# Attention head of a fused attention and bilinear FFN kernel: loads of v taken from ScalarE's queue ahead of its first copy, and two casts of k given to VectorE

## The chip, the cores and the metric

The kernel runs on one core of a Trainium2 chip. The metric is the device time of one execution in microseconds (us); the kernel before has a median of 317.13 us over five runs (315.9 to 317.66). The engines are named as in the profile: PE is TensorE (PEld its weight loads), DVE is VectorE, ACT is ScalarE, POOL is GpSimd and SP is SyncE. SP and ACT each have a queue of their own on which they issue transfers; "SPq" and "ACTq" mark an issue.

## What is computed

Attention within chunks of 64 tokens, and a bilinear feed-forward network on what it gives:

```python
# q, k, v: (8 batches, 8 heads, 576 tokens, 64)
scores = scale * q_c @ k_c.T                  # per chunk of 64 tokens: 64 x 64
attn = exp(scores - max) / sum
out = attn @ v_c
x = out.transpose(0, 2, 1, 3).reshape(4608, 512)
return (x @ w_a) * (x @ w_b) @ w_out          # w_a, w_b: 512 x 1536; w_out: 1536 x 512
```

All inputs and the output are float32; the kernel multiplies in bf16.

## The kernel before

The 4608 tokens are cut into nine blocks of 512, and a block into two units of 256 tokens. The attention of a unit gives a slice of `xT` (512 features by 256 tokens, bf16). The FFN of a block K then runs over 12 slices of 128 hidden features: for each, four matmuls with `wb` and four with `wa` (L398), a copy of one product by ScalarE (L409) and the product of both by VectorE (L410). After the 12 slices come the output products (L420, or L479 with fewer multiplications from block 2 on). The attention of later units is threaded between the slices of earlier blocks. TensorE's order, and that of every engine, is the order in which the program is written (`manual_schedule`); nothing is moved by a scheduler.

The first block has nothing ahead of it to hide behind, so its attention is the head of the program, and it is written out by hand (L550 to L653). It is cut by heads, not by tokens: four pairs of heads m = 0 to 3, for all 512 tokens of the block. Unit 0 of the head holds heads 0 to 3 (pairs 0 and 1), unit 1 heads 4 to 7. For each pair:

- `load_quads(m, x, ...)` (L137; the transfer's line is L140) brings q (x = 0) or k (x = 1) of the pair, 256 KB in float32, into `f32`.
- `quad_cast(m, x, eng)` (L303, recorded at L169) casts it to bf16 in `qkb`, a tile of 128 x 512.
- `quad_turn(m, x, eng)` (L311) transposes it on TensorE (four matmuls, L317) into one of the four PSUM banks `F`, and `eng` copies it to `qkT` (ScalarE's copies are recorded at L167, the others at L169).
- `quad_scores(m)` (L331; L340) makes the scores in the PSUM tile `PS`, `expo(hu, mm)` (L245) their exponential in `E`.

For each unit, `half_sums` (L351) adds up the exponentials, `half_log` (L361) and `half_inverse` (L365) turn the sums into reciprocals on ScalarE, `half_values` (L374) multiplies with v, and `half_normalise` (L384) on VectorE writes `xT`. v is loaded by `load_half_v(hu, gs, eng)` (L145; L147), 128 KB for each of four groups g of 128 tokens, and cast on GpSimd by `cast_v` (L185; two pieces for unit 0, four for unit 1). The casts of the weights follow v's on GpSimd. `fill` (L535; L539) issues matmuls on zeros whose result is not used.

What sets the order around the change:

- ScalarE issues its transfers from the same instruction stream in which its copies and exponentials stand. Before, that stream is: four loads of k, the activation table, v of unit 0 for g = 1 and 3, the copy of pair 0's q (first evacuation), v of unit 1 for g = 1 and 3, the exponential of pair 0, the copy of pair 2's q, the exponential of pair 1, and so on. SyncE issues four loads of q, v of units 0 and 1 for g = 0 and 2, then the weights.
- Loads tell their end by eight semaphores taken in turn, in the order of the program text over both queues. A load that takes a semaphore again waits, in its engine's stream, until the load that held it has landed. So before, ScalarE's v loads wait for: k of pair 1 (g = 1), k of pair 2 (g = 3), and for unit 1 the second and third v load of SyncE. SyncE's four v loads wait for k and q of pair 0, q of pair 1 and q of pair 2.
- TensorE's scores of pair 1 wait for the exponential of pair 0 as well as for their own operands, because both pairs write the same PSUM tile.

Of the kernel before, what the change touches and what calls it, by code (L numbers as in the profile page):

```python
# [11 lines left out]
def kernel(  # L12
# [10 lines left out]
    nc = tc.nc  # L23
# [84 lines left out]
    def nextF():  # L108
        return ring("f", F)
# [35 lines left out]
    def load_half_v(hu, gs, eng):  # L145
        for g in gs:
            eng.dma_start(  # L147
                out=f32[hu][2][:, g * 256:(g + 1) * 256].rearrange("p (h d) -> p h d", h=4),
                in_=v[0, 4 * hu:4 * hu + 4, g * 128:(g + 1) * 128, :].transpose([1, 0, 2]),
            )  # L150
# [14 lines left out]
    def copy(eng, out, in_):  # L165
        if eng is nc.scalar:
            eng.copy(out=out, in_=in_)  # L167
        else:
            eng.tensor_copy(out=out, in_=in_)  # L169
# [15 lines left out]
    def cast_v(u, eng, pieces=1):  # L185
        n = 1024 // pieces
        for i in range(pieces):
            copy(eng, vb[u % 3][:, n * i:n * i + n], f32[u % NF32][2][:, n * i:n * i + n])
# [53 lines left out]
    def expo(u, h=None):  # L242
        e = E[u % 2]
        s = slice(0, 512) if h is None else slice(h * 256, h * 256 + 256)
        nc.scalar.activation(out=e[:, :, s], in_=PS[:, :, s], func=AF.Exp, scale=scale)  # L245
# [57 lines left out]
    def quad_cast(m, x, eng):  # L303
        c = (m % 2) * 512
        copy(
            eng,
            qkb[m // 2][:, x, c:c + 512].rearrange("p (r h d) -> p h r d", r=4, h=2),
            f32[m // 2][x][:, c:c + 512].rearrange("p (h r d) -> p h r d", h=2, r=4),
        )

    def quad_turn(m, x, eng):  # L311

        t = nextF().bitcast(BF16)
        c0 = (m % 2) * 512
        for r in range(4):
            c = r * 128
            nc.tensor.transpose(  # L317
                t[:, c:c + 128], qkb[m // 2][:, x, c0 + c:c0 + c + 128], identity
            )
        n = 8 * x + 4 * (m % 2)  # L320
        dst = qkT[m // 2][:, n:n + 4, :]
        if x == 0:
            copy(eng, dst, t[:, 0:512].rearrange("p (r t) -> p r t", r=4))
        else:
            copy(
                eng,
                dst.rearrange("p a b -> p (a b)").rearrange("p (t r) -> p t r", r=4),
                t[:, 0:512].rearrange("p (r t) -> p t r", r=4),
            )

    def quad_scores(m):  # L331
        hu, mm = m // 2, m % 2
        tq = qkT[hu][:, 4 * mm:4 * mm + 4, :]
        tk = qkT[hu][:, 8 + 4 * mm:12 + 4 * mm, :].rearrange("p a b -> p (a b)")
        for g in range(4):
            c = mm * 256 + g * 64
            for j in range(2):
                for cl in range(2):
                    n = 2 * g + cl
                    nc.tensor.matmul(  # L340
                        PS[cl * 64:cl * 64 + 64, j, c:c + 64].rearrange("p (t r) -> p r t", r=4),
                        tk[j * 64:j * 64 + 64, n * 64:n * 64 + 64],
                        tq[j * 64:j * 64 + 64, :, n * 16:n * 16 + 16],
                        start=True,
                        stop=True,
                    )
# [188 lines left out]
    def fill(times, bank=None, n=512):  # L535


        for _ in range(times):
            nc.tensor.matmul(  # L539
                PA[:, 0, 0:n] if bank is None else bank[:, 0:n],  # L540
                zero[:, 0:128],
                zero[:, 0:n],
                start=True,
                stop=True,
            )
# [4 lines left out]
    with tc.manual_schedule():  # L550
# [4 lines left out]
        V, A, G = nc.vector, nc.scalar, nc.gpsimd  # L555
# [7 lines left out]
                name=nc.get_next_instruction_name(), act_func_set_id=6, ins=[], outs=[]  # L563
            )
        )
        for hu in range(2):
            load_half_v(hu, (0, 2), nc.sync)
        load_half_v(0, (1, 3), nc.scalar)

        def queue_half(i, h):  # L570
            for n, src in (("b", moe_w_b), ("a", moe_w_a)):
# [28 lines left out]
        fill(2)  # L600
        quad_cast(0, 0, V)
        quad_turn(0, 0, A)
        load_half_v(1, (1, 3), nc.scalar)
        quad_cast(0, 1, V)
        quad_turn(0, 1, V)
        fill(1, n=128)
        for m in range(1, 4):
            for x in range(2):
                quad_cast(m, x, G)
        cast_v(0, G, 2)  # L610
        cast_v(1, G, 4)
        for h in range(2):
# [6 lines left out]
        quad_turn(2, 0, A)  # L619
        quad_scores(1)  # L620
        expo(0, 1)
        quad_turn(2, 1, V)
        quad_turn(3, 0, V)
        half_sums(0, PA)
# [269 lines left out]
```

## Time and profile before

| What | us |
|---|---|
| median of five runs | 317.13 (315.9 to 317.66) |
| the profiled execution | 318.66 |
| its span, first to last instruction | 316.9 |
| TensorE busy | 307.3, 97% of the span |
| VectorE, ScalarE, GpSimd busy | 185.9, 133.9, 124.7 |
| first exponential begins | 10.51 |
| first of the FFN's matmuls in the chain of waits | 20.85 |
| granted TensorE clock at half, in the head | 8.89 to 22.54 |

The profile is of one execution. A row of its timeline gives start and duration in us, engine and line, operation, the tiles written and read with their sizes, the count, and in brackets how long the engine had stood idle before and what released it. A row of the chain of waits gives start, duration and what ran. A row of the table by stretches gives the stretch, its length, the busy time of PE, PEld, DVE, ACT and POOL with counts, the granted clock (1.00 is full speed), the share of the DMA engines and GB/s.

### The profile page before, as it was taken

What the parts mean: (1) busy time and instruction counts of PE and PEld (TensorE: products, weight loads), DVE (VectorE), ACT (ScalarE), POOL (GpSimd) and SP (SyncE); (2) the same over time, 40 slices, a digit from 0 to 9 for tenths busy, and PEclk for the clock granted to TensorE, in tenths of its full rate; (3) what the DMA queues carried; (4) which work ended last, traced back from release to release, by engine and by line L of the source; (5) the groups of instructions that cost most, each with busy time, mean ns of one, the idle gap of its engine ahead of it and who ended that gap; (6) DMA issues with size and microseconds to landing.
All of it is one profiled execution on the core that took longest, in us unless ns stands there. A gap on an engine that the chain in (4) does not pass through costs nothing.

```text
span 316.9 us, 7288 instructions
## 1 busy us (share of the span) xinstructions
PE 307.3 (97%) x2902; PEld 179.0 (56%) x2902; DVE 185.9 (59%) x369; ACT 133.9 (42%) x227; POOL 124.7 (39%) x161
## 2 busy tenths in 40 slices
PE   5799999999999999999999999999999999999995
PEld 2544445784444477446744674467446744674474
DVE  2334434553536874977486758765876476646663
ACT  1543325744524551644164416451645164413320
POOL 3678868978352116600650065006600400040023
PEclk9559999999999999999999999999999999999999
DMA  7999999999999778999299439962700210021003
GB/s 261 325 383 396 373 262 225 234 265 266 210 199 258 168 168 207 221 256 241 107 243 235 91 84 210 222 153 99 168 2 0 92 46 0 3 92 40 2 0 133
DMA packets 145842, 55.00 MB, mean 174 GB/s; under 512 B 126224, under 2 KB 139792, under 8 KB 145808
## 3 DMA queue, kind: packets, MB, share of 16 engines
q1 hardware_dynamic: 142608, 52.97, 66.6%
q10 hardware_dynamic: 3200, 1.57, 1.7%
q8 instruction: 22, 0.36, 0.5%
q14 instruction: 12, 0.10, 0.1%
HBM read 37.75 MB, written 9.44 MB: 149 GB/s over the span
## 4 chain that ended last, share of the span: by engine, by line
PE 93%; ACT 2%; DMA 2%; POOL 0%; ACTq 0%; issue 0%; POOLq 0%; DVEq 0%; DVE 0%
PE F L398 60%; PE F L479 19%; PE F L420 6%; DMA f<-in_k_dram 2%; PE F L251 2%; PE PS L234 2%; PE PA L267 1%; PE F L539 1%; PE F L317 1%; ACT E L245 1%; ACT qkT L167 0%; POOL part L497 0%; PE PS L340 0%; ACT lns L277 0%; ACT inv L281 0%; ACT inv L365 0%
## 5 line engine op out<-in xcount | busy, mean ns | idle before, releaser
L398 PE MATMUL F<-xT,wb 128*128 128x512 bf16 (+1 forms) x460 | 113.1, 368 | 0.0
L398 PE MATMUL F<-xT,wa 128*128 128x512 bf16 (+1 forms) x460 | 112.9, 367 | 0.0
L409 ACT CAST bsb<-F 128x512 bf16<-128x512 f32 (+1 forms) x115 | 64.2, 559 | 107.0 <-PE F L398 106.8
L410 DVE TENSOR_TENSOR ab<-F,bsb 128x512 bf16<-128x512 f32 (+1 forms) x115 | 75.3, 656 | 51.9 <-PE F L398 44.2
L398 PEld LDWEIGHTS <-wa 128*128 128x128 bf16 x460 | 45.2, 98 | 48.9 <-issue 0.8
L398 PEld LDWEIGHTS <-wb 128*128 128x128 bf16 x460 | 43.7, 98 | 44.6 <-issue 0.7
L497 POOL TENSOR_TENSOR part<-part 128x256 f32<-128x256 f32 x14 | 10.2, 725 | 133.9 <-ACT part L523 132.9
L169 POOL CAST qkb<-f 128x1024 bf16<-128x1024 f32 (+1 forms) x37 | 35.8, 982 | 27.4 <-DMA f<-in_k_dram 16.6
L479 PEld LDWEIGHTS <-wst 128*128 128x128 bf16 x420 | 41.1, 98 | 4.7
L479 PE MATMUL F<-wst 128*128 128x256 bf16 x252 | 33.3, 273 | 0.0
L286 DVE TENSOR_TENSOR xT<-PA,inv 128x512 bf16<-128x512 f32 x32 | 21.8, 684 | 16.6 <-ACT inv L281 16.6
L497 DVE TENSOR_TENSOR osb<-F,part 128x256 f32<-128x256 f32 x56 | 22.3, 420 | 11.0 <-POOL part L497 9.4
L497 POOL TENSOR_TENSOR part<-part,osb 128x256 f32<-128x256 f32 x28 | 19.7, 726 | 11.4 <-DVE osb L497 11.3
L169 POOL CAST vb<-f 128x1024 bf16<-128x1024 f32 (+2 forms) x22 | 19.9, 911 | 10.3 <-DMA f<-in_v_dram 10.3
L479 PE MATMUL F<-wst,ab 128*128 128x256 bf16 x168 | 22.8, 273 | 0.0
L277 ACT ACTIVATE lns<-F 128x512 f32<-128x512 f32 x32 | 17.4, 595 | 10.8 <-PE F L251 10.8
L420 PE MATMUL F<-wo,ab 128*128 128x512 bf16 x96 | 21.9, 379 | 0.0
L468 DVE TENSOR_TENSOR wst<-ab 128x512 bf16<-128x512 bf16 x42 | 21.8, 518 | 0.0
L467 DVE TENSOR_TENSOR wst<-ab 128x512 bf16<-128x512 bf16 x42 | 20.9, 498 | 0.0
L245 ACT ACTIVATE E<-PS 128x1024 bf16<-128x1024 f32 (+1 forms) x20 | 18.9, 943 | 4.7 <-PE PS L234 2.5
L479 PE MATMUL F<-wo,wst 128*128 128x256 bf16 x168 | 20.6, 273 | 0.0
L497 DVE TENSOR_TENSOR part<-F,part 128x256 f32<-128x256 f32 x15 | 6.4, 425 | 21.4 <-POOL part L497 21.4
(52 smaller groups left out, 201.9 us busy)
## 6 DMA issues: line engine op xcount, KB each, us to landing
out_dram<-osb SPq DMA_DIRECT2D x31, 256.0 KB, 2.3
f<-in_q_dram SPq DMA_DIRECT2D x28, 256.0 KB, 4.2
f<-in_v_dram SPq DMA_DIRECT2D x28, 256.0 KB, 4.2
f<-in_k_dram SPq DMA_DIRECT2D x24, 256.0 KB, 4.1
wst<-in_moe_w_out_dram SPq DMA_DIRECT2D x6, 512.0 KB, 8.9
wst<-in_moe_w_b_dram SPq DMA_DIRECT2D x5, 512.0 KB, 8.4
wst<-in_moe_w_a_dram SPq DMA_DIRECT2D x5, 512.0 KB, 7.8
f<-in_v_dram SPq DMA_DIRECT2D x12, 128.0 KB, 3.5
```

The lines of the kernel that those rows point to most:

```text
L169: eng.tensor_copy(out=out, in_=in_)
L245: nc.scalar.activation(out=e[:, :, s], in_=PS[:, :, s], func=AF.Exp, scale=scale)
L277: nc.scalar.activation(out=lns[:, cl, :], in_=SU[cl], func=AF.Ln)
L286: nc.vector.tensor_tensor(out=x.rearrange("p m (g c t) -> p c g m t", g=2, c=2)[:, cl], in0=PA[:, cl, :].rearrange(shape, g=2, m=4), in1=i ...
L398: nc.tensor.matmul(bank[:, 0:n], w[ft // 2][ft % 2][:, kt, :], x[:, kt, us[0] * 256:us[0] * 256 + n], start=(kt == 0), stop=(kt == NKT - 1),)
L409: nc.scalar.copy(out=bT[:, 0:n], in_=banks[0][:, 0:n])
L410: nc.vector.tensor_tensor(out=ab[ft][:, us[0] * 256:us[0] * 256 + n], in0=banks[1][:, 0:n], in1=bT[:, 0:n], op=MULT)
L420: nc.tensor.matmul(o, ab[ft][:, tg * 128:(tg + 1) * 128], wo[ft // 2][:, ft % 2, :], start=(ft == 0), stop=(ft == NFT - 1),)
L467: nc.vector.tensor_tensor(out=y[:, 0:2], in0=a[:, 0:2], in1=a[:, 2:4], op=ADD)
L468: nc.vector.tensor_tensor(out=y[:, 2:4], in0=a[:, 1:3], in1=a[:, 0:4:3], op=SUB)
L479: nc.tensor.matmul(o, a(i)[:, c:c + 128], b(i), start=(i == 0), stop=(i == NP - 1))
L497: eng.tensor_tensor(out=out, in0=in0, in1=in1, op=op)
```

## The change

Four edits, all in the head:

- SyncE loads v of unit 0 for g = 0 and 1 (before 0 and 2) and then all of unit 1's v (before g = 0 and 2), ahead of the weights. It has two loads more.
- ScalarE's two loads of unit 0's v ahead of its first copy are gone. Its two loads behind that copy are now unit 0's g = 2 and 3 (before unit 1's g = 1 and 3).
- k of pair 1 is cast by VectorE, behind its copy of pair 0's k, not by GpSimd.
- k of pair 3 is cast by VectorE, behind its copy of pair 1's k and ahead of its copy of pair 2's k.

The semaphores move along: SyncE's six v loads now wait for k and q of pair 0, k and q of pair 1, k and q of pair 2, in that order; ScalarE's g = 2 waits for q of pair 3, and its g = 3 for unit 0's g = 1, the second v load of SyncE. The first weight still waits for k of pair 3. TensorE's stream is the same.

```diff
-        for hu in range(2):
-            load_half_v(hu, (0, 2), nc.sync)
-        load_half_v(0, (1, 3), nc.scalar)
+        load_half_v(0, (0, 1), nc.sync)
+        load_half_v(1, range(4), nc.sync)
...
         fill(2)
         quad_cast(0, 0, V)
         quad_turn(0, 0, A)
-        load_half_v(1, (1, 3), nc.scalar)
+        load_half_v(0, (2, 3), nc.scalar)
         quad_cast(0, 1, V)
         quad_turn(0, 1, V)
         fill(1, n=128)
-        for m in range(1, 4):
-            for x in range(2):
-                quad_cast(m, x, G)
+        quad_cast(1, 1, V)
+        for m, x in ((1, 0), (2, 0), (2, 1), (3, 0)):
+            quad_cast(m, x, G)
         cast_v(0, G, 2)
         cast_v(1, G, 4)
...
         quad_scores(1)
         expo(0, 1)
+        quad_cast(3, 1, V)
         quad_turn(2, 1, V)
         quad_turn(3, 0, V)
```

## The prediction

> **What bounds the kernel now.** I read the page's slices first, then the chain of waits in order of time, then the timelines of ScalarE, TensorE, VectorE and GpSimd from 0 to 21 us, then a table of busy time by stretches cut where the granted clock changes.
>
> ```profile
> PE   5799999999999999999999999999999999999995
> PEclk9559999999999999999999999999999999999999
> ```
>
> TensorE is full in all slices (7.9 us each) but the first two and the last, and its clock is low in slices two and three. So a change to the head of the program can only pay by letting the dense stream start earlier.
>
> ```profile
> 1.79 5.77 DMA f<-in_k_dram
> 7.58 0.38 ACTq L147
> 8.00 0.60 ACT qkT L167
> 8.64 0.46 PE PS L340 x16
> 9.10 1.41 PE F L317 x12
> 10.51 0.61 ACT E L245
> 11.16 0.64 PE PS L340 x16
> ...
> 19.70 1.15 PE F L539 x2
> 20.85 21.62 PE F L398 x96
> ```
>
> The chain runs through two ScalarE pieces that stand behind loads: the first evacuation (L167, 8.00) behind a load's issue (7.58), and the first exponential (L245, 10.51). From 11.16 on it goes on through ScalarE's exponentials and logarithms to the stream at 20.85.
>
> ```profile
> 5.78 2.17 ACTq L147 DMA_DIRECT2D f<-in_v_dram  x2
> 8.00 0.59 ACT L167 COPY qkT<-F 128x512 bf16<-128x512 bf16 x1 [3.88 <-DMA f<-in_k_dram]
> 9.40 1.06 ACTq L147 DMA_DIRECT2D f<-in_v_dram  x2
> 10.51 0.60 ACT L245 ACTIVATE E<-PS 128x512 bf16<-128x512 f32 x1 [1.92 <-PE F L317]
> ```
>
> On ScalarE both are queued behind two issues of v (7.58 + 0.38 = 7.96, then the copy; 10.09 + 0.37 = 10.46, then the exponential). The releaser "PE F L317" of the exponential is misleading: its scores ended at 9.10.
>
> ```profile
> 8.64 0.46 PE L340 MATMUL PS<-qkT 64*64 64x64 bf16 x16 [2.50 <-ACT qkT L167]
> 11.16 0.64 PE L340 MATMUL PS<-qkT 64*64 64x64 bf16 x16 [0.67 <-ACT E L245]
> ```
>
> TensorE lost 2.50 us to the first and 0.67 us to the second. The second matters more than it looks: the scores of pair 1 wait for the first exponential, so whatever is won at 8.64 must also be won at 10.51.
>
> **The change, part by part.**
>
> First evacuation. Its transposes end at 5.63. With no load ahead, it runs at about 5.68 to 6.27 (0.59). The scores also need VectorE's evacuation of k (5.89 + 0.69 = 6.58), so they start at about 6.65, not 8.64: 2.0 us earlier. This is the visible gain, but not yet the gain of the chain.
>
> First exponential. Behind the evacuation ScalarE now has two issues, each with a wait on a semaphore used again: v of heads 0 to 3, rows 256 to 383, waits for the last q; rows 384 to 511 waits for the second v load of SyncE's queue. The last q landed just before GpSimd cast it at 8.34. The second v load was issued at 4.76 and landed 4.6 us later, 9.38 (ScalarE's issue at 9.40 in the fence waited for just that place in SyncE's queue). After the change that place is still second, issued at the same time, so I take 9.38 again. The second issue is then 9.40 to 9.84 (0.44), and the exponential starts at 9.89 instead of 10.51: 0.62 us earlier. Before, one more issue followed at 10.09 behind the third v landing; that is all that goes. So 2.0 us shrinks to 0.62: a new wait, of ScalarE on its own load, takes the place of the old one. Queued behind it are this exponential and the evacuation of pair 2's q; TensorE waits for the first.
>
> Scores of pair 1. They start 0.05 us after the exponential: 9.89 + 0.60 + 0.05 = 10.54 against 11.16. Their other inputs are earlier: transposes at 7.2 to 8.2, VectorE's two evacuations (0.43 and 0.69) end near 8.9.
>
> Two casts on VectorE.
>
> ```profile
> 9.67 1.12 DVE L169 COPY qkT<-F 128x512 bf16<-128x512 bf16 x2 [3.08 <-PE F L317]
> 12.38 1.02 DVE L169 COPY qkT<-F 128x512 bf16<-128x512 bf16 x2 [1.59 <-PE F L317]
> ```
>
> ```profile
> 4.05 0.43 DVE L169 CAST qkb<-f 128x512 bf16<-128x512 f32 x1 [2.58 <-DMA f<-in_q_dram]
> ```
>
> The same cast took 0.43 us. k of pair 1 fits at 6.6 to 7.0, k of pair 3 (landed near 8.5) at 8.9 to 9.3, both in holes of 3.08 and 1.59 us; in time nothing waits. The Trainium skill speaks against it: the page SBUF — State Buffer, section "A bandwidth-pool intuition that's wrong (but worth ruling out)", says that a VectorE cast in a two-port mode and GpSimd exclude each other, the later one waiting for the whole of the earlier. The trace agrees at 43.18, where such a cast of 512 columns took 0.95 us beside a GpSimd cast of 42.82 to 43.86. By the lone row the two casts cost 0.86 us of VectorE; by the rule up to 1.9 us, and a GpSimd cast (0.62) may wait 0.43. Even so the first ends by 7.6 and the second by 9.9, ahead of 10.54 and of pair 2's evacuation at 12.38 - 0.62 = 11.76. Cost zero either way; were the holes filled, 0.43 to 0.95 each.
>
> GpSimd loses two casts of 0.56 us pitch, then waits for v. It gains nothing on the chain.
>
> Loads. Landings before follow the order of issue over both queues: ScalarE's v of 5.78 landed at 10.4, after the three SyncE had issued by 5.60. Six v loads now precede on SyncE's queue and the first weight is issued near 8.7 (8.50 before). Each v load takes some 0.45 us (8.93 to 9.38). ScalarE's last v is issued at 9.42, where before an issue of 9.40 landed 3.9 us later; one more v load is ahead of it, so 13.3 + 0.45 = 13.75. Its cast ends at 14.4. The values of heads 0 to 3 begin at 15.48 and reach that half eight matmuls on, at 15.60; now 15.60 - 0.62 = 14.98. Cover 0.6 us; beyond it each us late is a us lost. The other v casts and the first weights follow on GpSimd, first weight about 0.9 us later (15.7, before 14.80); the stream, whose first matmul was issued at 20.64, needs it at 20.02. Cover over 4 us, price 1 to 1 if gone. Later weights wait for a memory queue that holds the same bytes: no cost.
>
> The 0.62 us then passes through the ScalarE chain (12.70 on) and the dense stream. No later wait of TensorE in the chain is on a transfer.
>
> **The clock**, which sets how much of it is kept.
>
> ```profile
> 5.47:8.89 3.42, 0.92 (x24) 0.82 (x22) 0.69 (x1) 0.59 (x1) 2.92 (x5) 1.00 1.13 355
> 15.71:19.13 3.42, 3.10 (x46) 1.06 (x38) 1.29 (x2) 2.55 (x6) 1.94 (x4) 0.50 1.09 380
> 19.13:22.54 3.41, 3.41 (x39) 1.83 (x40) 1.29 (x2) 0.51 (x1) 2.82 (x5) 0.50 1.09 385
> ```
>
> The clock fell to 0.50 after a stretch with TensorE busy 0.92 of 3.42 us, and returned at 22.54 after one with 3.41 of 3.41; 3.10 of 3.42 did not suffice. If the return stays at 22.54, the 0.62 us are spent at half speed and only 0.31 remains. The skill's page TensorE: Matmul & The Clock Gate, section "What's actually happening", says the window runs freely, not from the kernel's start. By the row alone, 0.31; by the rule, over many executions the return moves with the work, by 0.62 on average. The five times before spread over 1.76 us, as 3.41 / 2 = 1.71 us of such luck would give. I take 0.62.
>
> **Sum.** Profiled execution: 318.66 us, span 316.9, so 1.8 around it; it lies 1.5 above the median of 317.13, which I use. 317.13 - 0.62 = 316.51, its own range 316.1 to 316.9.
>
> **Rivals.**
>
> A, the new wait is short: the second v lands early and only VectorE's evacuation (8.9) holds the scores of pair 1. Gain up to 2.2, less 0.2 for v's half: 2.0, 315.1. Against it: 9.38 for that place in the queue. Chance 0.10.
>
> B, the clock helps more. With values and sums 0.62 earlier, the idle in 15.71 to 19.13 shrinks from some 0.3 to 0.15 us. If that window counts as full, the stream from 20.02 runs at full speed: 2.52 us of work by 22.54 instead of 1.90 / 2 = 0.95, gain 1.57, about 315.5. If the fuller window of 5.47 to 8.89 (some 1.8 us busy) keeps the clock up throughout, the fillers (1.02 us a pass, 0.85 early on) shrink too, near 2.5: 314.6. Chance 0.22.
>
> C, slower: v's second half. If ScalarE's load is served behind SyncE's weights through the first of 512 KB (landed 16.5, 17.0 with one v more), it lands at 17.4, is cast at 18.1 and holds the values 3.1 us beyond 14.98; net +2.5, 319.6. It costs from a landing at 14.3 on and eats the gain at 14.9. Against it: the 9.40 issue landed before a weight issued at 9.46 (4.5 us). Chance 0.10.
>
> D, nothing moves: the second v lands 0.6 later than before, and the exponential stays at 10.5: 317.1. Chance 0.08.
>
> **Numbers.** The forecast has 0.50. A measurement here can tell about 0.3%, 0.95 us, from no change. A, B and a 0.08 tail of the forecast are beyond it: faster 0.40. The rest of the forecast and D: 0.50. C: 0.10. The range 314.9 to 317.6 leaves out C and B's far end.
>
> **What would show it.** First evacuation near 5.7; first scores near 6.65; then a hole on TensorE until 10.5; ScalarE's second v issue near 9.4 and the exponential at 9.9; v's half cast by 14.4; the stream's first matmul near 20.0; the clock's return at 19.1 or 22.5. An exponential at 7 to 9 speaks for A, a cast after 15 for C.

## The result, and the profile after

| | median us | runs | ratio to before, 95% interval |
|---|---|---|---|
| before, same chip | 317.57 (315.81 to 319.09) | 75 | |
| after | 316.37 (315.3 to 317.96) | 40 | 0.9965 [0.9954, 0.9976] |
| after, repeated later | 317.28 | 22 | 0.9991 [0.9973, 1.0009] |

The first comparison has the change 1.2 us ahead, the repeat 0.3 us (0.0009 x 317.5). All executions whose granted clock is on record (211 of before, 61 of after; one of after at 321.38, a slow one, is left out) have means of 317.51 and 316.73: a gain of 0.78 us, standard error 0.12. With the 75 of before in the first row it is 0.81. That error takes the executions as independent, but the two sets of after differ by 0.61 in their means (standard error 0.22), so the true uncertainty is larger. The forecast was 0.62. How one kernel can come out at 0.35% and at 0.09% is the second half of this text.

The profiled execution of after took 315.5 us, with a span of 313.7. Its slices:

```profile
PE   7599999999999999999999999999999999999995
...
PEclk9799999999999999999999999999999999999999
```

TensorE's busy slices are the same but for the first two (75 for 57). What differs most is the clock row: it begins 9799 where before stood 9559. This execution had a single stretch of half clock, the profiled one of before four. So its chain, in order of time, must be read with care from the values (L374, 14.80) on, since they run at another clock than before; the part that matters lies ahead of them:

```profile
4.79 4.71 DMA f<-in_v_dram
...
9.52 0.43 ACTq L147
...
10.00 0.61 ACT E L245
...
10.65 0.64 PE PS L340 x16
...
18.44 2.69 PE F L398 x12
```

The first evacuation and the first scores have left the chain. It now comes straight from SyncE's second v load (issued 4.79, landed 9.50) through ScalarE's issue to the first exponential. ScalarE's and TensorE's timelines show the same from their side:

```profile
5.69 0.59 ACT L167 COPY qkT<-F 128x512 bf16<-128x512 bf16 x1 [1.57 <-PE F L317]
8.26 1.70 ACTq L147 DMA_DIRECT2D f<-in_v_dram  x2
10.00 0.60 ACT L245 ACTIVATE E<-PS 128x512 bf16<-128x512 f32 x1 [3.72 <-DMA f<-in_v_dram]
```

```profile
6.87 0.42 PE L340 MATMUL PS<-qkT 64*64 64x64 bf16 x16 [0.25 <-DVE qkT L169]
...
10.65 0.64 PE L340 MATMUL PS<-qkT 64*64 64x64 bf16 x16 [2.58 <-ACT E L245]
```

The evacuation went from 8.00 to 5.69 and the first scores from 8.64 to 6.87, but the exponential only from 10.51 to 10.00. In the brackets, the 2.50 us that TensorE lost ahead of the first scores are gone, and 2.58 us stand ahead of the second: the hole has moved by one step. The releaser is now named rightly, "DMA f<-in_v_dram".

The two casts and what waits for v:

```profile
6.73 0.42 DVE L169 CAST qkb<-f 128x512 bf16<-128x512 f32 x1
...
8.59 0.60 DVE L169 CAST qkb<-f 128x512 bf16<-128x512 f32 x1
11.87 1.02 DVE L169 COPY qkT<-F 128x512 bf16<-128x512 bf16 x2 [2.68 <-PE F L317]
```

```profile
13.73 2.00 POOL L169 CAST vb<-f 128x512 bf16<-128x512 f32 x5 [3.49 <-DMA f<-in_v_dram]
15.68 0.61 POOL L169 CAST wb<-wst 128x512 bf16<-128x512 f32 x1
```

Both casts lie ahead of a hole of 2.68 us. v's second half is cast from 13.73 on; the values began at 14.80 and waited for nothing. At last the clock, in the table by stretches:

```profile
6.85:10.26 3.41, 1.21 (x28) 1.03 (x29) 1.83 (x4) 0.26 (x1) 2.44 (x4) 1.00 1.21 318
10.26:13.68 3.42, 3.03 (x48) 2.05 (x47) 1.02 (x2) 2.21 (x4) 0.00 (x0) 0.50 1.20 315
13.68:17.09 3.41, 1.91 (x56) 1.00 (x54) 1.98 (x3) 2.84 (x6) 3.36 (x8) 1.00 1.10 365
```

The clock fell after 1.21 us busy of 3.41, came back after 3.03 of 3.42, and stayed at full after 1.91 of 3.41. Before, 3.10 of 3.42 had not brought it back.

One sentence of the description above is not quite right: the loads take the semaphores in turn, but not in the plain order of the text over the two queues. In that order ScalarE's two loads of after, which stand behind eight loads of weights in the text, would wait for the first two of these. The waits named there agree with the landings in the traces (9.50 us for the second v load, ScalarE's issue at 9.52).

### The profile page after: what moved, and what is told of

The parts are those of the page before. It is cut to its first block, busy times and chain, and to the rows that moved or that the text cites. A ratio compares the mean times of both kernels' runs of the same rounds, so it can differ in the third digit from the quotient of the medians.

```text
span 313.7 us, 7288 instructions
## 1 busy us (share of the span) xinstructions
PE 304.1 (97%) x2902; PEld 177.5 (57%) x2902; DVE 185.0 (59%) x371; ACT 134.0 (43%) x227; POOL 123.4 (39%) x159
## 4 chain that ended last, share of the span: by engine, by line
PE 92%; DMA 3%; ACT 2%; POOL 0%; issue 0%; POOLq 0%; DVEq 0%; ACTq 0%; SPq 0%; DVE 0%
PE F L398 60%; PE F L479 19%; PE F L420 6%; PE F L251 2%; PE PS L234 2%; DMA f<-in_v_dram 2%; PE PA L267 1%; DMA f<-in_k_dram 1%; PE F L539 1%; ACT E L245 1%; POOL part L497 0%; ACT lns L277 0%; ACT inv L281 0%; ACT inv L365 0%; ACT lns L361 0%
## 5 line engine op out<-in xcount | busy, mean ns | idle before, releaser
L169 POOL CAST qkb<-f 128x1024 bf16<-128x1024 f32 (+1 forms) x35 | 34.6, 1001 | 33.2 <-DMA f<-in_k_dram 19.9
L169 POOL CAST vb<-f 128x1024 bf16<-128x1024 f32 (+2 forms) x22 | 19.8, 912 | 9.8 <-DMA f<-in_v_dram 9.8
L467 DVE TENSOR_TENSOR wst<-ab 128x512 bf16<-128x512 bf16 x42 | 20.9, 498 | 0.0
L468 DVE TENSOR_TENSOR wst<-ab 128x512 bf16<-128x512 bf16 x42 | 20.1, 478 | 0.0
L497 DVE TENSOR_TENSOR part<-F,part 128x256 f32<-128x256 f32 x15 | 6.4, 425 | 21.4 <-POOL part L497 21.4
```

Source lines behind the costliest of these rows:

```text
L467: nc.vector.tensor_tensor(out=y[:, 0:2], in0=a[:, 0:2], in1=a[:, 2:4], op=ADD)
L468: nc.vector.tensor_tensor(out=y[:, 2:4], in0=a[:, 1:3], in1=a[:, 0:4:3], op=SUB)
L497: eng.tensor_tensor(out=out, in0=in0, in1=in1, op=op)
```

## The experiments

The theory: a load's issue in ScalarE's stream waits for the landing of SyncE's second v load, and that alone holds the first exponential; the casts do nothing; the rest of the gain is the clock. The rivals: the casts give or cost something; the load queue has nothing to do with it and the clock does it all; v's late half costs something.

### The parts, and v wholly on SyncE

These four ran on one chip against 72 runs of before (median 317.5). First the kernel before itself, as a measure of the scatter.

> The kernel before once more, to see the granted clock of each of its executions beside those of the changed kernel (40 executions: 8 with a mean clock of 0.995, 16 with 0.989, 16 with 0.981 to 0.984). Queue theory (the gain is ScalarE's shorter wait alone, 0.5 us in the profile; the rest is chance): ratio 1.000 and the same mix of clocks. Clock theory (the rest of the 1.1 us is fewer half-speed stretches of 3.4 us): ratio 1.000, and most executions at 0.977 to 0.984, few or none at 0.995.

Measured: 317.52, ratio 0.9988 [0.9966, 1.001]; exponential at 10.55 and the stream's first matmul at 20.58 in an execution with three stretches at half clock. So the exponential's time repeated within 0.04 us here, while the interval is as wide as the effect that is sought.

`loads_only` has the change without the two casts:

```diff
-        quad_cast(1, 1, V)
-        for m, x in ((1, 0), (2, 0), (2, 1), (3, 0)):
-            quad_cast(m, x, G)
+        for m in range(1, 4):
+            for x in range(2):
+                quad_cast(m, x, G)
...
-        quad_cast(3, 1, V)
```

> The change's loads alone: v's loads as in the changed kernel, all casts of k on GpSimd as before. Queue theory and clock theory: the whole gain, ratio 0.9965, first exponential at 10.0, since the casts on GpSimd end by 9.5, ahead of the scores of pair 1. Cast theory (the two casts on VectorE are needed for part of it): a ratio nearer to 0.998.

Measured: 316.91, ratio 0.9977 [0.996, 0.9994], exponential at 10.17. The interval holds both what the queue theory and what the cast theory expected. `casts_only` has the loads of before and the two casts on VectorE (the other half of the same diff).

> The change's casts alone: k of pairs 1 and 3 cast by VectorE, all loads as before. Queue theory and clock theory: no change, ratio 1.000, first exponential at 10.5. Cast theory: part of the gain, about 0.998.

Measured: 317.5, ratio 0.9995 [0.9977, 1.0013]. The exponential came at 10.96 where 10.5 was expected: ScalarE's second pair of issues began at 9.88, against 9.40 and 9.51 in the two traces of before. Whether this is scatter of the landings or comes of the casts, one trace cannot tell. In the medians the gain goes with the loads; the casts alone do nothing that can be seen.

`v_on_sync` takes the last of v from ScalarE's stream:

```diff
-        load_half_v(0, (0, 1), nc.sync)
+        load_half_v(0, range(4), nc.sync)
...
-        load_half_v(0, (2, 3), nc.scalar)
```

> The changed kernel with its last two ScalarE loads moved too: all eight v loads on SyncE ahead of the weights, none on ScalarE. It takes away the wait that the forecast put in the place of the old one. Queue theory: the first exponential follows the first scores, at 7.3 to 7.4, the scores of pair 1 then wait for VectorE's evacuation, about 8.9 instead of 10.65; v of heads 0 to 3 lands by 10.5 instead of 13.7. Gain over the changed kernel 1.7 us, ratio to before 0.991, the clock's part on top. Rival (GpSimd's and VectorE's casts hold the later pairs, or the weights come late): gain over the changed kernel under 0.7 us, ratio 0.994 or more.

Measured: 316.07, ratio 0.9954 [0.9931, 0.9976]. ScalarE's timeline:

```profile
5.69 0.59 ACT L167 COPY qkT<-F 128x512 bf16<-128x512 bf16 x1 [1.58 <-PE F L317]
7.34 0.60 ACT L245 ACTIVATE E<-PS 128x512 bf16<-128x512 f32 x1 [1.06 <-PE PS L340]
...
9.20 0.60 ACT L245 ACTIVATE E<-PS 128x512 bf16<-128x512 f32 x1 [0.50 <-PE PS L340]
```

With no issue behind the copy, the exponential runs at 7.34 instead of 10.00 and waits for its scores, as it should: the issue is the cause. The stream's first matmul comes at 17.97, 2.7 us ahead of the 20.64 of before. The time gained is 1.4 us in the medians, and only some 0.35 beyond the changed kernel (0.9954 against 0.9965): the exponential came as the queue theory expected, the time as its rival did. Part of the rest is found later in the execution, where TensorE waits for tiles that a DMA transposes for a later unit's attention (the columns: who waits for what, us in all, times, the longest):

```profile
PE PS L234 <- DMA qkT<-qkb: 1.0, 2, 0.5
```

In the trace of after, TensorE waits for nothing between 60 and 110 us. Here the chain from 62.80 to 75.59 runs through two transfers (a v load of 6.21 us, a transposing one of 6.58) and only then through TensorE.

### The clock by itself, a load fewer, and the issue behind the exponential

The next four ran against 71 runs of before (median 317.4). `before_fill` is the kernel before with one filler pass more, which keeps TensorE busy in the first hole and leaves ScalarE's path as it was:

```diff
         fill(1, n=128)
+        fill(1)
         for m in range(1, 4):
```

> The kernel before with one more filler matmul of 512 columns in TensorE's hole of 2.5 us ahead of the first scores (two passes, 1.7 us at full clock, 2.0 at half, done by 8.2, ahead of 8.64). No load, cast or wait changes. Clock theory: the hole no longer drops the clock in most executions, the mean granted clock rises from 0.984 to 0.99 or more, and the time falls by 0.5 to 1.2 us, ratio 0.996 to 0.998, though the first exponential stays at 10.5. Queue theory: nothing on ScalarE's path moves, ratio 1.000.

Measured: 316.82, ratio 0.9976 [0.9958, 0.9994]. The exponential is at 10.53, unmoved. So some 0.6 us (0.2 to 1.3 by the interval) come without any change on ScalarE's path, and the mean granted clock is 0.992, against 0.987 in the 71 of before. The table by stretches, with the borders set by the drop at 15.35 and the length of 3.41:

```profile
5.11:8.52 3.41, 1.76 (x18) 1.03 (x20) 0.69 (x1) 0.59 (x1) 2.50 (x5) 1.00 1.11 358
8.52:11.94 3.42, 1.91 (x52) 1.65 (x51) 1.02 (x2) 1.37 (x3) 2.15 (x4) 1.00 1.23 308
11.94:15.35 3.41, 2.03 (x76) 1.39 (x74) 1.92 (x4) 2.90 (x6) 2.02 (x6) 1.00 1.18 338
15.35:18.76 3.41, 2.93 (x34) 0.98 (x37) 1.08 (x2) 2.54 (x5) 2.38 (x5) 0.50 1.09 380
```

1.76 and 1.91 us of 3.41 kept the clock up where 0.92 had not before; but 2.03, more than these, did not keep it. So there is no sharp border by this measure of busy time.

`after_fill` has the same pass in the hole that the change leaves:

```diff
+        fill(1)
         quad_scores(1)
```

> The changed kernel with one filler matmul of 512 columns in its hole of TensorE from 8.1 to 10.6, ahead of the scores of pair 1 (done by 10.2). Clock theory: the mean granted clock rises from 0.988 to 0.993 or more and the time falls by 0.4 to 0.8 us beyond the changed kernel, ratio to before 0.994 to 0.995; the first exponential stays at 10.0. Queue theory: as the changed kernel, 0.9965.

Measured: 316.12, ratio 0.9964 [0.9946, 0.9981], exponential at 9.93. The mean clock rose to 0.994 as the clock theory expected, but the ratio is that of the queue theory, 0.9964 for 0.9965. Against the repeat of the changed kernel below (0.9991, on the same chip) it would be a gain, so what the filler is worth here is not settled. The mean spans of the filled pair are 314.95 and 314.33 us, 0.62 apart (standard error 0.26). That is no measure of the loads' part alone, because the clocks differ too: 0.9922 and 0.9943 are 0.4 of a half-speed stretch apart, by the count explained below.

`one_v` leaves one v load on ScalarE, so that its wait is for q of pair 3 and not for v:

```diff
-        load_half_v(0, (0, 1), nc.sync)
+        load_half_v(0, (0, 1, 2), nc.sync)
...
-        load_half_v(0, (2, 3), nc.scalar)
+        load_half_v(0, (3,), nc.scalar)
```

> Between the changed kernel and the one with all v loads on SyncE: ScalarE keeps only the last load of unit 0's v, whose semaphore waits for q of pair 3 (8.2), not for a v load. Queue theory: the first exponential at 8.3 + 0.4 = 8.7, the scores of pair 1 at 9.35, the FFN stream 1.3 us earlier than in the changed kernel, ratio about 0.993 if nothing later holds it. Rival (a later wait on transfers takes the gain back, as the wait of TensorE for transposed tiles at 60 us and later did with all v loads on SyncE): no more than 0.5 us beyond the changed kernel, 0.995 or more.

Measured: 316.04, ratio 0.9958 [0.9938, 0.9977]. ScalarE's timeline:

```profile
8.57 0.45 ACTq L147 DMA_DIRECT2D f<-in_v_dram  x1
9.07 0.60 ACT L245 ACTIVATE E<-PS 128x512 bf16<-128x512 f32 x1 [2.79 <-DMA f<-in_q_dram]
```

The scores of pair 1 are at 9.72, the stream at 18.96: the exponential follows the issue that stands ahead of it, whatever that waits for, here a load of q. The time is again the rival's (0.995 or more), not the 0.993 of the queue theory. But its trace has no wait of TensorE for transposed tiles between 60 and 110 us; where the time went is told below, with the clock.

`exp_first` puts both issues behind the exponential, where the second exponential stands behind them:

```diff
-        load_half_v(0, (2, 3), nc.scalar)
         quad_cast(0, 1, V)
         quad_turn(0, 1, V)
+        quad_scores(0)
+        expo(0, 0)
+        load_half_v(0, (2, 3), nc.scalar)
...
-        quad_scores(0)
-        expo(0, 0)
```

> The changed kernel with ScalarE's two v loads behind the first exponential instead of ahead of it. Their semaphores then wait for the second and the fourth v load of SyncE. Queue theory: the first exponential at 7.3, but the copy of pair 2's q and the second exponential stand behind the issues, near 10.8 and 11.4 (11.34 in the changed kernel), so the wait only moves on by one instruction; v's half lands about 0.8 us later, is cast after 15 and holds the values of unit 0 by 0.3 us or so: ratio 0.997 to 0.999. Rival (only the first exponential counts): 2.7 us of gain, 0.989.

Measured: 318.26, ratio 1.0022 [1.0007, 1.0037], slower than before; the expectation (0.997 to 0.999) missed. ScalarE's, GpSimd's and TensorE's timelines:

```profile
6.63 0.60 ACT L245 ACTIVATE E<-PS 128x512 bf16<-128x512 f32 x1 [0.85 <-PE PS L340]
10.00 1.28 ACTq L147 DMA_DIRECT2D f<-in_v_dram  x2
11.32 0.59 ACT L167 COPY qkT<-F 128x512 bf16<-128x512 bf16 x1 [4.10 <-DMA f<-in_v_dram]
11.80 0.60 ACT L245 ACTIVATE E<-PS 128x512 bf16<-128x512 f32 x1
```

```profile
16.24 2.00 POOL L169 CAST vb<-f 128x512 bf16<-128x512 f32 x5 [5.52 <-DMA f<-in_v_dram]
```

```profile
16.91 0.54 PE L374 MATMUL PA<-E,vb 64*64 64x64 bf16 x24 [1.32 <-POOL vb L169]
```

The first exponential is early (6.63), but the second comes at 11.80, since the issues now stand between the two, and v's half is cast at 16.24 only, so that the values stop for 1.32 us, where 0.3 was expected. This is the price that the prediction's rival C names, though v is late here because it is issued late, not because the weights are served first. The change as made stayed clear of it in its own trace.

### The change again, its loads again, and the best of both

These ran against 46 runs of before (median 317.58). The first is the changed kernel, unaltered; the second is `loads_only` once more.

> The changed kernel once more, beside the loads alone on the same chip. All theories: ratio 0.9965, give or take 0.0015; mean granted clock 0.988 as in the first 40 executions.

Measured: 317.28, ratio 0.9991 [0.9973, 1.0009], which missed the expectation; mean granted clock 0.9856 for the 0.988 expected; exponential at 9.95, the stream's first matmul at 19.82 with three stretches at half clock.

> The loads alone once more. The first time they gave 0.9977 with the changed kernel's 0.9965 inside the interval, and a mean span of 315.05 against 314.72. Queue and clock theory: the same as the changed kernel on the same chip within 0.001. Cast theory: 0.001 or more above it again.

Measured: 316.75, ratio 0.9975 [0.9956, 0.9994]. On one chip the change without its casts is not behind the change with them: the casts add nothing that can be seen. The trace of the loads alone has something else: v's second half is cast at 14.44 only (13.73 in the trace of after), and the values stop for it for 0.30 us.

`one_v_fill` is `one_v` with a filler of half the length:

```diff
+        fill(1, n=256)
         quad_scores(1)
```

> The best of both: one v load left on ScalarE (0.9958) and a filler matmul of 256 columns in TensorE's hole ahead of the scores of pair 1 (0.85 us at full clock, from 8.1 to 9.0, ahead of the exponential's end near 9.6). Clock theory: mean granted clock above the 0.990 of that kernel, time 0.2 to 0.5 us below it, ratio 0.994 to 0.995. Rival (the head is no longer what counts): 0.9958 again.

Measured: 315.92, ratio 0.9933 [0.991, 0.9956], the lowest of all, though its interval overlaps those of `one_v`, `v_on_sync` and `after_fill`. Its table by stretches:

```profile
5.25:8.67 3.42, 2.45 (x40) 1.78 (x38) 2.05 (x4) 0.59 (x1) 1.98 (x4) 1.00 1.11 358
8.67:12.08 3.41, 2.31 (x49) 1.50 (x48) 1.90 (x4) 2.67 (x5) 1.51 (x3) 1.00 1.23 270
12.08:15.49 3.41, 1.99 (x54) 1.07 (x54) 1.73 (x3) 2.81 (x7) 2.28 (x7) 1.00 1.05 310
```

The clock never falls, and the stream's first matmul comes at 16.47. Yet this execution's span is 314.9, because TensorE's waits between 60 and 110 us now have this line:

```profile
PE PS L234 <- DMA qkT<-qkb: 2.8, 2, 2.6
```

Two thirds of the 4.2 us won at the head (20.64 - 16.47) are given back there in this execution.

### The clock over many executions

Each execution has a mean granted clock. A stretch of 3.41 us at half speed takes 3.41 x 0.5 / 316 = 0.0054 off it, so the mean tells how many such stretches there were (the profiled execution of before, with four, has 0.977; that of after, with one, 0.995). Number of executions and their mean span in us:

| half-speed stretches (mean clock) | before | after | loads alone |
|---|---|---|---|
| four (below 0.980) | 54: 316.93 | 2: 316.95 | 0 |
| three (to 0.9865) | 103: 315.56 | 27: 315.46 | 25: 315.42 |
| two (to 0.992) | 21: 314.34 | 20: 314.43 | 11: 314.50 |
| one, or part of one (to 0.999) | 17: 316.06 | 12: 314.27 | 3: 313.70 |
| none (1.000) | 16: 314.09 | 0 | 0 |

Read along a row, the kernels take the same time within 0.16 us wherever they have over ten executions, except in the row of one stretch. Read down a column, each half-speed stretch beyond two costs 0.9 to 1.5 us; from two to none, before gains only 0.25. So the gain shows as a shift between rows: four stretches in 26% of the executions before, in 3% after. From the mean clocks (0.9848 and 0.9871) before had 2.82 such stretches and after 2.39; in the repeat alone after had 2.67 (0.9856), in the first comparison 2.24 (0.9879). The same kernel thus differed by 0.4 of a stretch between two sets of runs. At 0.9 to 1.5 us each, that is most of the 0.6 us between the two sets.

The number of stretches is not all: it matters where they lie. In the head, low clock is partly hidden in waits (TensorE was busy 2.74 and 2.62 of 3.41 us in the first two slow stretches of before). Once the stream has begun TensorE is full (3.41 of 3.41), and each microsecond at half speed should cost half a microsecond. The thirteen traces of this study agree with that. In each, the span is the start of the stream's first matmul, plus half of the time for which the clock stays low after it, plus the later waits for transposed tiles, plus a rest of 294.9 to 295.6 us, whose spread of 0.7 us is not explained here. Seven of them, in us; the time of full clock is read from the granted clock in steps of 0.3 us:

| | stream starts | full clock again | half of the slow time after the start | span | rest |
|---|---|---|---|---|---|
| before | 20.64 | 22.54 | 0.95 | 316.9 | 295.3 |
| `b_again` | 20.58 | 20.0 | 0 | 315.6 | 295.0 |
| after | 18.28 | 13.68 | 0 | 313.7 | 295.4 |
| `after_again` | 19.82 | 19.5 | 0 | 315.1 | 295.3 |
| `after_fill` | 19.82 | 21.4 | 0.8 | 315.6 | 295.0 |
| `one_v` | 18.96 | 20.8 | 0.9 | 314.8 | 294.9 |
| `v_on_sync` (and 1.0 of waits) | 17.97 | 19.8 | 0.9 | 315.2 | 295.3 |

So in these executions of `one_v`, `v_on_sync` and `after_fill` the clock fell later than before (at 12.9 to 14.5 us, against 8.89), came back after the stream had begun, and took back 0.8 to 0.9 us of what the head had won. And `b_again` and `after_again`, with three stretches each and none of their slow time behind the start of the stream, differ by 0.76 us in that start and by 0.5 us in the span.

## Why the prediction was right or wrong

**First evacuation and first scores.** Right: 5.69 for 5.68, and 6.87 for 6.65; the scores were 0.2 us late because VectorE's evacuation began at 6.12, not 5.89.

**First exponential.** Right: 10.00, and 9.95 in the repeat, for 9.89. SyncE's second v load landed at 9.50 for the 9.38 taken. In five traces with the change's loads on record it lies between 9.91 and 10.17. That the 2.0 us shrink to about half a us is shown both ways: `v_on_sync` without the issue ran it at 7.34, and `one_v` with an earlier wait at 9.07. Rivals A and D are out: the wait is not short, and the exponential did move. Scores of pair 1: 10.65 for 10.54.

**The casts.** Right at zero, by `casts_only` and by `loads_again` beside `after_again`. The rule that the prediction took from the Trainium skill's page SBUF — State Buffer (section "A bandwidth-pool intuition that's wrong (but worth ruling out)") is seen in part. The first cast took 0.42 like the prediction's lone row, though a cast of GpSimd (6.97 to 7.62) began in its last 0.18 us. The second began at 8.59, beside GpSimd casts that ended at 8.92, and took 0.60; waiting for the whole of them would have made it 0.76 (0.33 + 0.43), an estimate by the page's rule. The row at 43.18 lies short of the rule by the same 0.16 us (0.95, for 0.68 + 0.43). Neither mattered, because both casts lie ahead of a hole of 2.68 us.

**v's second half and the weights.** Right: cast from 13.73 for a landing of 13.75, first weight's cast at 15.68 for 15.7. That the landing was met to 0.02 us is in part luck: with the same loads v was cast at 13.26 in the repeat and at 14.44 in `loads_again`, where the cover of 0.6 us was gone and the values waited 0.30 us. Rival C did not happen, and `exp_first` shows what v costs when its cast comes 2.5 us later: 1.32 us of waiting.

**No later wait on a transfer.** Right for this change, by the waits of 60 to 110 us. It is no general truth of the kernel: with 2.7 us won TensorE waits 1.0 us there, with 4.2 us won 2.8 us.

**The clock.** Here a term was mis-sized. The prediction kept 0.62 us, on the rule of the Trainium skill's page TensorE: Matmul & The Clock Gate (section "What's actually happening") that the window runs freely, and put into rival B, as another outcome with a chance of 0.22, that the fuller stretches hold the clock up. The rule agrees with the traces: stretch borders lay at 5.47, 6.85, 5.11 and 5.25 us in four executions, so the phase differs from one to the next. But B is not another outcome; it is the same program in another phase. The stream was foreseen near 20.0 and the clock's return at 19.1 or 22.5; the profiled execution of after has 18.28 and 13.68, the repeat's 19.82 and 19.5. The sum should have been the queue's part plus what the fuller window saves on average. By a shift alone, 0.5 us earlier would save 0.5 / 3.41 = 0.15 stretches; all executions together saved 0.43, the repeat alone 0.15. `before_fill` shows that filling one hole can be worth 0.6 us on its own.

Measured, the whole is 0.78 us where 0.62 was foreseen. What share of it is the queue's is not shown. For a share near the forecast speak the first exponential, 0.51 to 0.60 us earlier, and the 0.5 us between the spans of `b_again` and `after_again`. Against it, executions of both kernels with the same number of slow stretches take the same time within 0.16 us. So the wait on ScalarE was foreseen rightly and the path to the stream is right, but that the time came so near to 0.62 is in part luck.

**The base.** The five times of before had a median of 317.13, the 75 of 317.57. The forecast of 316.5 lies beside the 316.37 measured partly by luck: this 0.44 us and the larger gain of the first comparison offset each other.

**What stays open.** How much of the 1.2 us in the first comparison was luck of the phase, and how much the fuller stretches; between 1.2 and the repeat's 0.3 the runs give only the pooled figure. By what measure the clock is judged is open too. And 16 executions of before with a mean clock of 0.997 or 0.998, part of one slow stretch, took 316.0 to 316.5 us, 2 us more than those with none (314.09). That they lose it to the transposing transfers, as `one_v_fill` did, is a guess from that one trace; no trace of theirs was kept.

## What to carry to other kernels

When a load is moved behind a piece of work in an engine's stream, look at the landing that its issue waits for: the next piece of work inherits that wait, and the gain is the difference of the two landings (here 0.5 us of the 2.0 at first sight). Holes in a short head can cost twice, as time and as clock: a filler in one was worth 0.6 us before, nearly as much as the whole change, though what it is worth in the changed kernel is not settled. Low clock costs most behind the start of the dense stream. Where the clock's phase is free, compare mixes over dozens of executions before a few tenths of a per cent are put down to an edit, and after winning microseconds at the head look for the transfer that is late next.

## What the runs showed of the hardware

The granted clock dropped after stretches of 3.41 us with TensorE busy 0.92 (before) and 1.21 us (after), held after 1.76 and 1.91 (`before_fill`) and 1.99 (`one_v_fill`), but dropped after 2.03 (`before_fill`) and 2.02 (`one_v`, 10.50 to 13.93). It returned after 3.03 busy (after), and not after 3.10 (before) or 2.93 (`before_fill`). So neither border is a plain share of the busy time that the profile shows.

An issue of v itself took 0.37 to 0.43 us in after (8.26 and 9.52) and in `exp_first` (10.00 and 10.91). The rest of a row with two issues, 1.70 us in after and 1.28 in `exp_first`, is waiting between them: 0.89 and 0.47 us.
